# A new order, other PSUM banks and three rewritten steps in the opening of an attention and two-MLP kernel

## The chip, the cores and the metric

The kernel runs on one core of a Trainium2 chip, in one launch. The metric is device time in microseconds: the time from the start to the end of one execution. Before the change the median of three executions is 849.32 us (847.17 to 850.44).

## What is computed

```python
a = exp(phi - max(phi, axis=2))            # maximum over the sequence
a = a / (sum(a, axis=2) + 1e-9)            # (4, 8, 576, 32)
k_m = einsum('bhsm,bhsd->bhmd', a, k)      # 32 memory slots for each head
v_m = einsum('bhsm,bhsd->bhmd', a, v)
scores = q @ k_m.T / 8                     # (4, 8, 576, 32)
attn = softmax(scores)                     # over the 32 slots
x = (attn @ v_m), heads side by side       # (2304, 512)
h = x @ w_in;  x = (h * sigmoid(h)) @ w_out        # 512 -> 2048 -> 512
out = ((x @ w_a) * (x @ w_b)) @ w_out2             # 512 -> 1536 -> 512
```

q, k, v are (4, 8, 576, 64) and phi is (4, 8, 576, 32), all float32. The weights come as 64-bit floats and are turned into float32 on the chip. The large products are made of three float32r products each, of a high and a low half of both operands.

## The kernel before

The work runs in stages. The **opening** does the attention of the four batches and the first units of the first MLP; then follow the rest of the first MLP, and the second MLP (`ab`, `op`). In the opening a hand-written planner sets the order: each task is a generator that yields its next operation with an engine, an estimated time, what it needs and which buffers it takes or frees. The planner always takes, on the engine that can start first, the operation of the lowest rank that is ready by then. The instructions of each engine keep the order that comes out, and each engine works through its own queue in that order. Ranks are 0 for the loads, 1 for what follows a unit's products, 2 to 8 by batch and weight tile, 8.5 for the units.

For a batch `b` the tasks of the opening are:

- `weights(b)`: phi arrives in tile `ph` (128 rows, 4 x 9 x 32 values a row). VectorE takes the maximum over the nine pieces with four `tensor_tensor` instructions (tiles `m`, `mxa`); TensorE transposes it (`mxt`), VectorE reduces that (`mx`), ScalarE widens it (`mb`), TensorE brings it back (`bc`), VectorE subtracts it (`ph<-ph,bc`), ScalarE takes the exponential.
- `sums(b)`: VectorE adds the nine pieces with four more instructions (`m`, `es`).
- `memory(b)`: TensorE multiplies the exponentials by k and v (`kvp`, 72 products a batch), and `es` by a column of ones (`sm`, 8 products). VectorE takes the reciprocals (`rec`), ScalarE scales (`kvn`); for batches 0 and 1 TensorE transposes the keys (`kt`).
- `values(b)`: the transposed values (`vt`), split into `vbd_hi` and `vbd_lo`.
- `turn(b, hg, n)`, batches 0 and 1: three transposes of the queries each (`qt`), copied by ScalarE to `qT`.
- `scores(b, hg)`: the products `sc`, and then the softmax, nearly all of it on VectorE (`x`, `mxq`, `smq`, `xt`), split at its end into the halves `at` (two tiles for each of the two `hg`; the low half is `at<-xt,at`).
- `vw_first`: the values times the first weights (`mp`), split into `m0h`, `m0l` and so on.
- the units: `hp` products of `at` with the tiles `m0h`, `m0l`, then `g`, `gh`, `gl`, then `yp` products with `wo`.
- `tile_of`: turns a weight tile into float32 with VectorE and ScalarE (`e`, `t`), then into a high half (ScalarE) and a low half (VectorE, `wi_0l`, `wo_0l`, ...).

PSUM is divided into pools of two buffers each: "bank" (`ps_t`: `mp`, `kvp`, `kt`, `vt`), "hp" and "yp". `BANK_W[b]` says from which pool `mxt`, `bc` and `sm` of a batch come, `BANK_Q[b]` the same for `qt`. A buffer is taken again when the instruction that reads it is done; a writer behind it waits. Loads go out on SyncE's queue in the order of `LOADS`; each waits there until its buffer is free, and what stands behind it waits too.

Of the kernel before, what the change touches and what calls it, by code (L numbers as in the profile page):

```python
# [9 lines left out]
F32 = mybir.dt.float32  # L10
# [4 lines left out]
ALU = mybir.AluOpType  # L15
AX = mybir.AxisListType
# [4 lines left out]
def attn_moe_moe2_kernel(  # L21
# [540 lines left out]

    def weights(b):

        yield op("V", 1750, [f"phi{b}"])
        e = st[b]["ph"]

        m4 = p_s.tile([128, 4, 4, NM], F32, tag="m4", name="m4")
        mxa = p_s.tile([128, 4, NM], F32, tag="mxa", bufs=2, name="mxa")
        for o, x, y in (  # L570
            (m4, e[:, :, 0:4], e[:, :, 4:8]), (m4[:, :, 0:2], m4[:, :, 0:2], m4[:, :, 2:4]),
            (m4[:, :, 0], m4[:, :, 0], m4[:, :, 1]), (mxa, m4[:, :, 0], e[:, :, 8]),
        ):
            V.tensor_tensor(out=o, in0=x, in1=y, op=ALU.max)
        yield op("T", 400, take=(BANK_W[b], f"mxt{b}"))
        mxt = bank_of(BANK_W[b], "mxt")[:, :128].rearrange("p (r n) -> p r n", r=2)
        T.transpose(mxt.rearrange("p r n -> p (r n)"), mxa.rearrange("p x m -> p (x m)"), ident)
        yield op("V", 290, free=[f"mxt{b}"])
        mx = p_s.tile([128, 2], F32, tag="mx", bufs=2, name="mx")
        V.tensor_reduce(out=mx, in_=mxt, op=ALU.max, axis=AX.X)  # L580

        yield op("A", 300)
        mb = p_s.tile([128, 2, 64], F32, tag="mxa", bufs=2, name="mb")
        A.activation(out=mb, in_=mx.unsqueeze(2).to_broadcast([128, 2, 64]), func=AF.Copy)
        yield op("T", 500, take=(BANK_W[b], f"bc{b}"))
# [7 lines left out]
    def sums(b):

        yield op("V", 1800, [f"w{b}"], done=f"es{b}")
        e = st[b]["ph"]
        m4 = p_s.tile([128, 4, 4, NM], F32, tag="m4", name="m4")
        es = st[b]["es"] = p_s.tile([128, 4, NM], F32, tag="mxa", bufs=2, name="es")
        for o, x, y in (
            (m4, e[:, :, 0:4], e[:, :, 4:8]), (m4[:, :, 0:2], m4[:, :, 0:2], m4[:, :, 2:4]),  # L600
            (m4[:, :, 0], m4[:, :, 0], m4[:, :, 1]), (es, m4[:, :, 0], e[:, :, 8]),
        ):
            V.tensor_tensor(out=o, in0=x, in1=y, op=ALU.add)

    def memory(b):

        t = st[b]
        for hg in range(2):
            yield op("T", 2070, [f"w{b}", f"kv{b}{hg}"], take=("bank", f"kvp{b}") if hg == 0 else None,
                     free=[f"kv{b}{hg}"] + [f"ph{b}"] * hg)  # L610
            e = t["ph"]
            if hg == 0:
                kvp = ps_t.tile([128, 2, 2 * D], F32, tag="t", name="kvp")
            kv = t.pop(("kv", hg))
            for c in range(JP):
                for h in range(4):

                    o = slice(32 * h, 32 * h + 32)
                    x, r = (h // 2 + b) % 2, slice(64 * (h % 2), 64 * (h % 2) + 64)
                    T.matmul(  # L620
                        kvp[o, hg], e[r, 2 * hg + x, c], kv[r, :, x, c * D : c * D + D], start=(c == 0), stop=(c == JP - 1)
                    )
        yield op("T", 250, [f"es{b}"], take=(BANK_W[b], f"sm{b}"))
        sm = bank_of(BANK_W[b], "sm")[:, :2]
        for hg in range(2):
            for h in range(4):
                x, r = (h // 2 + b) % 2, slice(64 * (h % 2), 64 * (h % 2) + 64)
                T.matmul(sm[32 * h : 32 * h + 32, hg : hg + 1], t["es"][r, 2 * hg + x], ones[r, :1])
        yield op("V", 350, free=[f"sm{b}"])
        rec = p_s.tile([128, 2], F32, tag="mx", bufs=2, name="rec")  # L630
        V.tensor_scalar_add(rec, sm, EPS)
        V.reciprocal(out=rec, in_=rec)
        yield op("A", 950, [f"vt{b - 1}"] if b else [], done=f"kvn{b}", take=("kvn", f"kvn{b}"), free=[f"kvp{b}"])

        kvn = t["kvn"] = p_s.tile([128, 2, 4, D], F32, tag="kvn", name="kvn")
        for hg in range(2):
            A.activation(
                out=kvn[:, hg].rearrange("p (a r) d -> p a r d", r=2),
                in_=kvp[:, hg, : 2 * D].rearrange("p (a d) -> p a d", a=2).unsqueeze(2).to_broadcast([128, 2, 2, D]),
                func=AF.Copy, scale=rec[:, hg : hg + 1],  # L640
            )
        if b in NEW:

            yield op("T", 500, done=f"kmT{b}", take=("bank", f"kt{b}"))
            kt = ps_t.tile([128, 2, 128], F32, tag="t", name="kt")
            for hg in range(2):
                T.transpose(kt[:, hg], kvn[:, hg, 0:2].rearrange("p a d -> p (a d)"), ident)
            yield op("A", 400, done=f"kT{b}", take=("kT", f"kT{b}"), free=[f"kt{b}"])
            t["kT"] = p_s.tile([128, 2, 128], F32, tag="kT", bufs=2, name="kT")
            A.activation(out=t["kT"], in_=kt, func=AF.Copy)  # L650
            return
        yield op("V", 350, done=f"kmT{b}")
        kmT = t["kmT"] = p_s.tile([128, 2, 2, NM], F32, tag="kmT", bufs=2, name="kmT")
        V.transpose(out=kmT.rearrange("p g e m -> p g (e m)"), in_=kvn[:, :, 0])
        yield op("A", 1250, [f"sc{b - 1}0", f"sc{b - 1}1"] if b > 2 else [], done=f"kbd{b}")
        for h in range(4):
            r = slice(32 * h, 32 * h + 32)
            A.activation(out=kbd[r, :, :, r], in_=kmT[r], func=AF.Copy)
# [94 lines left out]
    def tile_of(what, c):  # L753
# [26 lines left out]
        V.tensor_tensor(out=ti, in0=ti, in1=ei, op=ALU.add)  # L780
        yield op("A", 650, free=[f"e_{name}"])
        copy(A, hi, t)
        yield op("V", 700, done=name, free=[f"t_{name}"])
        V.tensor_tensor(out=lo, in0=t, in1=hi.bitcast(F32), op=ALU.subtract)
        (wi if what == "wi" else wo)[0, c] = hi, lo

    def loads():
# [78 lines left out]
    def feed_forward():  # L866
        for n, u in enumerate(UNITS):
# [3 lines left out]
            for c in range(4):  # L871
                if c < len(cs):
                    key = f"{n}_{c}"
                    rings["g"][1].append("gg" + key)
                    yield op("T", 800, [f"at{b}0", f"at{b}1", f"m{b}0{halves}", f"m{b}1{halves}"]
                             + ([("free", rings["g"][1][-9])] if len(rings["g"][1]) > 8 else []),
                             take=("hp", "hp" + key),
                             free=[f"m{b}0", f"m{b}1"] if last and c == len(cs) - 1 else [])
                    hp = mul_h(u, cs[c])
                    add(1, g_task(u, cs[c], hp, key), free_at["T"])  # L880
                if n:
                    w = UNITS[n - 1]
                    key = f"{n - 1}_y{c}"
                    yield op("T", 400 * len(w[3]), [f"g{n - 1}_{i}" for i in range(len(w[3]))] + [f"wo{i}" for i in w[3]],
                             take=("yp", key), free=[f"gg{n - 1}_{i}" for i in range(len(w[3]))] if c == 3 else [])
                    yp = mul_y(w, c)
                    add(1, y_task(w, c, yp, key), free_at["T"])
                tick()
                due(0)
            done.add((f, b, hf))  # L890
# [6 lines left out]


    LOADS = (
        "wi00 q00 phi00 wo00 kv00 wi01 q01 kv01 wo01 phi10 q10 wi02 kv11 kv10 q11 wi03 q20 wo03 phi20 wo02 q21 kv20 phi30 q30 kv21 q31 kv31 kv30"  # L900
    ).split()
    NEW = (0, 1)
    RANK = (2, 5, 7, 8)
    RANK_I = (3, 3, 5, 4)
    RANK_O = (4, 4, 2, 6)
    BANK_W = ("yp", "yp", "hp", "hp")
    BANK_Q = ("yp", "bank", "bank", "bank")
    fill()
    add(0, loads())
    add(8.5, feed_forward())  # L910
    for b in range(B):
        add(RANK[b], weights(b))
        add(RANK[b], memory(b))
        add(RANK[b], sums(b))
        add(RANK[b], values(b))
        for hg in range(2):
            for n in range(3 * (b in NEW)):
                add(RANK[b], turn(b, hg, n))
            add(RANK[b], scores(b, hg))
        for kc in range(2):  # L920
            if b == 0:
                add(3, vw_first(0, kc, (0,)))
                add(5, vw_first(0, kc, (1,)))
            else:
                add(RANK[b], vw_first(b, kc, (0, 1)))
    for c in range(4):
        add(RANK_I[c], tile_of("wi", c))
        add(RANK_O[c], tile_of("wo", c))
    run(range(9))
    run((1, 8.5))  # L930
    pinned[0] = False
    for p in (ps_sc, ps_t, ff["h"], ff["y"], p_c, p_s, p_in):
        p.release()
# [356 lines left out]
```

## Time and profile before

| | |
|---|---|
| median of three executions | 849.32 us |
| the profiled execution, its own time | 846.86 us |
| its span, first to last instruction | 845.1 us |
| TensorE busy (PE) | 804.0 us, 95% |
| VectorE busy (DVE) | 571.3 us, 68% |
| ScalarE busy (ACT) | 470.9 us, 56% |
| GpSimd busy (POOL) | 72.4 us, 9% |

The page's busy row for TensorE, in slices of about 21 us, is `6584989999...`: only the first seven slices or so are below nine tenths. The page's chain of work that ended last is TensorE for 84%. A share over the whole span says little about the opening, so the rows further down are of stretches and single instructions there. A row of the timeline gives the start, the duration, the engine, the operation, output <- inputs, shapes and a count; in brackets the idle time of the engine ahead of it and what ended it.

### The profile page before, as it was taken

How to read it: one execution, taken by the hardware profiler on the slowest of the kernel's cores; microseconds unless marked ns; L12 is line 12 of the kernel's file. 1: busy time of each engine (PE TensorE's matmuls, PEld its weight loads, DVE VectorE, ACT ScalarE, POOL GpSimd, SP SyncE). 2: the span in 40 equal slices, each digit the busy share in tenths (PEclk: the TensorE clock that was granted, in tenths of full speed). 3: DMA queues.
4: the chain of work that ended last, by engine and by line, in shares of the span. 5: the costliest groups of instructions: out<-in, count | busy, mean ns of one | idle time of the engine just before them, and what ended most of it. 6: DMA issues, size and time to landing. Idle time of an engine off the chain costs nothing.

```text
span 845.1 us, 14031 instructions
## 1 busy us (share of the span) xinstructions
PE 804.0 (95%) x5460; PEld 759.6 (90%) x5460; DVE 571.3 (68%) x1116; ACT 470.9 (56%) x947; POOL 72.4 (9%) x87
## 2 busy tenths in 40 slices
PE   6584989999999999999999999999999999999998
PEld 5374889999999999999989999999999999999996
DVE  5998776877677667767598886586664874543534
ACT  4574667996676567867456775645443553222220
POOL 1000000211010001122001101101010110100000
PEclk8697999999999999999999999999999999999999
DMA  9752601235331333355287779979785985756653
GB/s 338 218 205 78 224 1 51 75 101 126 100 88 38 85 92 88 79 121 116 41 318 249 249 236 284 256 251 266 219 238 159 279 234 162 195 178 200 198 157 75
DMA packets 59956, 140.91 MB, mean 167 GB/s; under 512 B 5233, under 2 KB 30321, under 8 KB 59889
## 3 DMA queue, kind: packets, MB, share of 16 engines
q1 hardware_dynamic: 48512, 122.44, 44.4%
q0 software_dynamic: 10224, 17.04, 12.0%
q8 instruction: 43, 0.70, 0.3%
q10 hardware_dynamic: 1152, 0.52, 0.3%
q14 instruction: 25, 0.20, 0.1%
HBM read 101.71 MB, written 21.23 MB: 145 GB/s over the span
## 4 chain that ended last, share of the span: by engine, by line
PE 84%; ACT 7%; DVE 6%; DMA 2%; issue 1%; ACTq 0%; DVEq 0%
PE ab L69 30%; PE yp L69 19%; PE op L69 18%; PE hp L69 9%; PE mp L69 3%; PE kvp L69 2%; PE sc L69 1%; ACT g L69 1%; ACT gh L69 1%; DVE t_wi L69 1%; DVE x L69 1%; DMA st_b<-in_moe_w_b_dram 1%; ACT L69 1%; ACT e_wo L69 1%; DVE smq L69 1%
## 5 line engine op out<-in xcount | busy, mean ns | idle before, releaser
L69 PE MATMUL ab<-yq,wh 128*128 128x384 f32 x1080 | 260.7, 338 | 2.0 <-DVE yq L69 1.2
L69 PEld LDWEIGHTS ab<-yq,wh 128*128 128x128 f32 x1080 | 196.5, 189 | 9.1 <-DVE yq L69 1.5
L69 PE MATMUL ab<-yq,wl 128*128 128x384 f32 x432 | 146.3, 339 | 0.0
L69 ACT ACTIVATE u<-ab 128x384 f32<-128x384 f32 x108 | 52.3, 490 | 87.1 <-PE ab L69 86.8
L69 DVE TENSOR_TENSOR gl<-g,gh 128x288 fp32r<-128x288 f32 x128 | 58.9, 464 | 47.2 <-ACT gh L69 46.5
L69 DVE TENSOR_TENSOR y<-op,y 128x512 f32<-128x512 f32 x54 | 37.3, 692 | 78.2 <-PE op L69 77.3
L69 PE MATMUL op<-wol,ph 128*128 128x512 f32 x216 | 85.5, 396 | 0.0
L69 ACT ACTIVATE g<-hp 128x288 f32<-128x288 f32 x128 | 51.9, 409 | 60.1 <-PE hp L69 52.1
L69 PE MATMUL op<-woh,pl 128*128 128x512 f32 x216 | 84.9, 393 | 0.0
L69 PE MATMUL op<-woh,ph 128*128 128x512 f32 x216 | 84.6, 392 | 0.0
L69 PEld LDWEIGHTS ab<-yq,wl 128*128 128x128 f32 x432 | 81.6, 189 | 0.0
L69 ACT ACTIVATE ph<-u 128x384 fp32r<-128x384 f32 x72 | 37.4, 524 | 66.0 <-DVE u L69 60.2
L69 DVE TENSOR_TENSOR u<-ab,u 128x384 f32<-128x384 f32 x108 | 59.8, 556 | 20.6 <-PE ab L69 19.6
L69 DVE TENSOR_TENSOR y<-yp,y 128x288 f32<-128x288 f32 x104 | 47.4, 456 | 29.2 <-PE yp L69 28.6
L69 ACT ACTIVATE gh<-g 128x288 fp32r<-128x288 f32 x128 | 55.9, 443 | 2.7
L69 PEld LDWEIGHTS op<-woh,pl 128*128 128x128 f32 x216 | 40.6, 188 | 9.0
L69 PEld LDWEIGHTS op<-woh,ph 128*128 128x128 f32 x216 | 40.6, 188 | 6.7
L69 PEld LDWEIGHTS op<-wol,ph 128*128 128x128 f32 x216 | 40.5, 188 | 6.4
L69 DVE TENSOR_TENSOR pl<-u,ph 128x384 fp32r<-128x384 f32 x72 | 39.2, 551 | 2.0 <-ACT ph L69 1.8
L69 PE MATMUL hp<-at,m0h 128*128 128x288 f32 x128 | 27.9, 309 | 11.1 <-DVE ph L69 11.1
L69 PE MATMUL yp<-gh,wo_0h 128*128 128x288 f32 x128 | 38.1, 298 | 0.3 <-ACT y L69 0.3
L69 PE MATMUL yp<-gh,wo_2h 128*128 128x288 f32 x128 | 38.1, 297 | 0.1
(218 smaller groups left out, 1887.5 us busy)
## 6 DMA issues: line engine op xcount, KB each, us to landing
yq<-yd SPq DMA_DIRECT2D x63, 768.0 KB, 4.8
yd<-yq SPq DMA_DIRECT2D x21, 768.0 KB, 4.4
st_wi<-in_moe_w_in_dram SPq DMA_DIRECT2D x16, 512.0 KB, 4.3
st_wo<-in_moe_w_out_dram SPq DMA_DIRECT2D x16, 512.0 KB, 3.8
st_a<-in_moe_w_a_dram SPq DMA_DIRECT2D x12, 512.0 KB, 6.1
st_b<-in_moe_w_b_dram SPq DMA_DIRECT2D x12, 512.0 KB, 5.6
wl<-s POOLq DMA_DIRECT2D x24, 256.0 KB, 6.1
st_o<-in_moe_w_out_dram SPq DMA_DIRECT2D x12, 512.0 KB, 6.0
```

What stands on the lines that cost most here:

```text
L69: ins = f(*a, **k)
```

## The change

- `weights`: the four maxima become one `tensor_reduce` over a rearranged view of `ph`, so that the nine pieces are read with a stride of 32 values.
- `sums` is gone. `memory` forms the sum with 72 products of the exponentials with the column of ones (`sm`), added up in PSUM over the nine pieces; `ph` is freed only behind them.
- `tile_of`: the low half of the four `wo` tiles of the opening is made by GpSimd; that of the `wi` tiles stays on VectorE.
- The ranks become a table `R` with a number of its own for each task, the order of the loads is another, and `BANK_W` and `BANK_Q` name other pools. All tasks, the ones after the units' products too, are run by one call.

```diff
-        for o, x, y in (
-            (m4, e[:, :, 0:4], e[:, :, 4:8]), (m4[:, :, 0:2], m4[:, :, 0:2], m4[:, :, 2:4]),
-            (m4[:, :, 0], m4[:, :, 0], m4[:, :, 1]), (mxa, m4[:, :, 0], e[:, :, 8]),
-        ):
-            V.tensor_tensor(out=o, in0=x, in1=y, op=ALU.max)
+        V.tensor_reduce(out=mxa, in_=e.rearrange("p x c m -> p x m c"), op=ALU.max, axis=AX.X)
...
-        yield op("T", 250, [f"es{b}"], take=(BANK_W[b], f"sm{b}"))
+        yield op("T", 1100, take=(BANK_W[b], f"sm{b}"), free=[f"ph{b}"])
         sm = bank_of(BANK_W[b], "sm")[:, :2]
         for hg in range(2):
-            for h in range(4):
-                x, r = (h // 2 + b) % 2, slice(64 * (h % 2), 64 * (h % 2) + 64)
-                T.matmul(sm[32 * h : 32 * h + 32, hg : hg + 1], t["es"][r, 2 * hg + x], ones[r, :1])
+            for c in range(JP):
+                for h in range(4):
+                    x, r = (h // 2 + b) % 2, slice(64 * (h % 2), 64 * (h % 2) + 64)
+                    T.matmul(
+                        sm[32 * h : 32 * h + 32, hg : hg + 1], e[r, 2 * hg + x, c], ones[r, :1],
+                        start=(c == 0), stop=(c == JP - 1), skip_group_check=True,
+                    )
...
-        yield op("V", 700, done=name, free=[f"t_{name}"])
-        V.tensor_tensor(out=lo, in0=t, in1=hi.bitcast(F32), op=ALU.subtract)
+        eng, ns, g = ("V", 700, V) if what == "wi" else ("G", 1500, GP)
+        yield op(eng, ns, done=name, free=[f"t_{name}"])
+        g.tensor_tensor(out=lo, in0=t, in1=hi.bitcast(F32), op=ALU.subtract)
...
-        "wi00 q00 phi00 wo00 kv00 wi01 q01 kv01 wo01 phi10 q10 wi02 kv11 kv10 q11 wi03 q20 wo03 phi20 wo02 q21 kv20 phi30 q30 kv21 q31 kv31 kv30"
+        "wo00 phi00 kv00 wi00 wi01 kv01 wo01 q00 phi10 q01 kv11 q11 wi03 wo03 q10 q21 kv10 wi02 phi20 kv21 q20 kv20 phi30 wo02 q31 q30 kv31 kv30"
...
-    RANK = (2, 5, 7, 8)
...
-    BANK_W = ("yp", "yp", "hp", "hp")
-    BANK_Q = ("yp", "bank", "bank", "bank")
...
+        weights=(44, 26, 4, 36), memory=(14, 0, 39, 41), values=(16, 33, 18, 21), turn0=(1, 35, 32, 8),
...
+    BANK_W = ("yp", "hp", "yp", "yp")
+    BANK_Q = ("yp", "yp", "hp", "bank")
```

What the new numbers do to the order, at three places. First TensorE, ahead of the first `hp` products (`at_67` and its like are the halves of batch 0's softmax; `qt` are the transposed queries, `bc` is the maximum of batch 1 on its way back, `sc` the scores of batch 0):

```order
 L69 MATMUL mp<-wi_1l,vbd_hi_83 128x256
 L69 MATMUL mp<-wi_1h,vbd_lo_85 128x256
-L69 MATMUL sc<-qT,kT 32x288 x8
-L69 MATMUL qt<-ident,qq 128x128 x9
+L69 MATMUL qt<-ident,qq 128x128 x12
+L69 MATMUL bc<-ident,mb 128x128
+L69 MATMUL qt<-ident,qq 128x128 x6
 L69 MATMUL hp<-at_67,m0h 128x288
 L69 MATMUL hp<-at_75,m0h 128x288
```

The scores have moved further ahead, and batch 1's `bc` and all its `qt` now stand ahead of the first `hp`. Right behind the first two groups of `hp`, TensorE too:

```order
 L69 MATMUL hp<-at_76,m0h 128x288
 L69 MATMUL hp<-at_68,m0l 128x288
-L69 MATMUL bc<-ident,mb 128x128
-L69 MATMUL qt<-ident,qq 128x128 x6
 L69 MATMUL kvp<-kv,ph 32x128 x72
+L69 MATMUL sm<-ones,ph 32x1 x72
+L69 MATMUL mxt<-ident,mxa 128x128
 L69 MATMUL mp<-wi_3h,vbd_hi_83 128x256
 L69 MATMUL mp<-wi_3l,vbd_hi_83 128x256
```

Batch 1's `kvp` follows `hp` at once, and the 72 products with ones follow `kvp`. The last place is VectorE at the end of batch 1's softmax, where batch 2's maximum is subtracted (`ph<-ph,bc`). Before:

```order
L69 TENSOR_TENSOR x<-x,smq 128x576 x2
L69 STREAM_TRANSPOSE xt<-x 128x576 x2
L69 TENSOR_TENSOR at_77<-xt,at_69 128x576
L69 TENSOR_TENSOR at_78<-xt,at_70 128x576
L69 TENSOR_TENSOR wo_3l<-t_wo_757,wo_3h 128x512
L69 TENSOR_TENSOR ph<-ph,bc 128x1152
L69 STREAM_TRANSPOSE qT<-qq 128x1152
```

and after the change:

```order
L69 TENSOR_REDUCE mx<-mxt 128x2
L69 TENSOR_REDUCE smq<-x 128x18
L69 TENSOR_SCALAR smq<-smq 128x18
L69 RECIPROCAL smq<-smq 128x18
L69 ISA t_wo_991<-t_wo_991,e_wo_977 128x1024
L69 TENSOR_TENSOR x<-x,smq 128x576
L69 TENSOR_TENSOR ph<-ph,bc 128x1152
L69 STREAM_TRANSPOSE xt<-x 128x576
```

The subtraction stood behind both low halves of batch 1's softmax (`at_77`, `at_78`); now it stands six rows behind batch 2's `mx`, ahead of both.

## Rows read from the trace of the kernel before

**Rows 1.** Busy times by stretch: engines, granted clock, DMA share, GB/s

```profile
0.00:76.40 76.40, 44.18 (x578) 37.01 (x579) 63.80 (x134) 43.23 (x89) 4.21 (x12) 0.82 0.64 210
76.40:130.00 53.60, 50.91 (x580) 46.75 (x581) 38.74 (x83) 34.46 (x69) 0.00 (x0) 0.94 0.37 119
130.00:400.00 270.00, 269.93 (x1981) 266.59 (x1980) 188.32 (x384) 196.80 (x420) 33.82 (x37) 1.00 0.37 89
```

**Rows 2.** Timeline of TensorE in the opening, single rows

```profile
0.97 4.57 PE L69 MATMUL jk<-ones 128*96 128x96 f32 x32 [0.97 <-POOL ones L69]
...
14.67 3.81 PE L69 MATMUL kvp<-kv,ph 64*32 64x128 f32 x72 [2.64 <-ACT ph L69]
...
20.02 2.17 PE L69 MATMUL kvp<-kv,ph 64*32 64x128 f32 x72
22.01 0.28 PE L69 MATMUL sm<-ones,es 64*32 64x1 f32 x16
...
38.43 2.38 PE L69 MATMUL qt<-ident,qq 128*128 128x128 f32 x9 [8.51 <-DVE m0l L69]
...
76.41 0.82 PE L69 MATMUL hp<-at,m0h 128*128 128x288 f32 x2 [11.09 <-DVE ph L69]
```

**Rows 3.** Timeline of VectorE in the opening, single rows

```profile
6.22 0.69 DVE L69 SCALAR_TENSOR_TENSOR t_wi<-e_wi,t_wi 128x512 uint32<-128x512 uint32 x1
...
8.24 0.69 DVE L69 TENSOR_TENSOR m<-ph 128x512 f32<-128x512 f32 x1
...
9.96 0.68 DVE L69 TENSOR_TENSOR wi_0l<-t_wi,wi_0h 128x512 fp32r<-128x512 f32 x1
...
22.69 0.15 DVE L69 TENSOR_SCALAR rec<-sm 128x2 f32<-128x2 f32 x1
...
26.18 0.72 DVE L69 TENSOR_TENSOR vbd_lo<-vt,vbd_hi 64x64 fp32r<-64x64 f32 x4
...
38.82 0.76 DVE L69 TENSOR_TENSOR at<-xt,at 128x576 fp32r<-128x576 f32 x1
...
74.92 1.35 DVE L69 TENSOR_TENSOR ph<-ph,bc 128x1152 f32<-128x1152 f32 x1
```

**Rows 4.** Busy times between the two softmaxes' ends, columns as in rows 1

```profile
39.60:74.50 34.90, 22.62 (x309) 19.88 (x307) 33.29 (x72) 24.72 (x52) 0.00 (x0) 0.89 0.40 133
```

**Rows 5.** Busy times in the slow-clock stretches; sums of the first three, the last two

```profile
31.80:41.90 10.10, 3.47 (x15) 3.13 (x16) 9.66 (x19) 4.23 (x8) 0.00 (x0) 0.50 0.44 96
sum 20.15, PE 10.88 PEld 8.69 DVE 18.30 ACT 8.59 POOL 0.00; mean PE 3.63 PEld 2.90 DVE 6.10 ACT 2.86 POOL 0.00
...
sum 6.40, PE 6.40 PEld 6.01 DVE 6.23 ACT 4.87 POOL 0.00; mean PE 3.20 PEld 3.00 DVE 3.11 ACT 2.43 POOL 0.00
```

**Rows 6.** DMA issues at 1.26 and 4.41 us: count, size, us to landing

```profile
qq<-in_q_dram SPq DMA_DIRECT2D x1, 576.0 KB, 4.7
...
qq<-in_q_dram SPq DMA_DIRECT2D x1, 576.0 KB, 10.3
```

**Rows 7.** Groups on VectorE, 0 to 130 us: count, busy us, mean ns, idle

```profile
L69 DVE TENSOR_REDUCE mxq<-x 128x18 f32<-128x576 f32 x8 | 5.9, 734 | 0.1
L69 DVE TENSOR_REDUCE mx<-mxt 128x2 f32<-128x128 f32 x4 | 1.1, 283 | 0.0
```

**Rows 8.** Chain of work that ended last: start, us, what; then TensorE's timeline

```profile
24.84 1.21 PE sc L69 x16
...
83.94 0.80 PE hp L69 x6
...
94.17 2.21 PE L69 MATMUL sc<-qT,kbd 128*128 128x288 f32 x8
```

**Rows 9.** Timelines of GpSimd and VectorE near 151 us, and a VectorE group

```profile
150.68 1.62 POOL L69 TENSOR_TENSOR wi_1l<-t_wi,wi_1h 128x512 fp32r<-128x512 f32 x1 [1.62 <-ACT wi_1h L69]
...
151.06 1.56 DVE L69 TENSOR_TENSOR gl<-g,gh 128x288 fp32r<-128x288 f32 x1
...
L69 DVE TENSOR_TENSOR gl<-g,gh 128x288 fp32r<-128x288 f32 x16 | 7.2, 452 | 2.1 <-ACT gh L69 1.8
```

More of the change, by code (lines that the diff above doesn't have):

```diff
@@ L563, in weights @@
     def weights(b):
-        yield op("V", 1750, [f"phi{b}"])
+        yield op("V", 1350, [f"phi{b}"])
         e = st[b]["ph"]
-        m4 = p_s.tile([128, 4, 4, NM], F32, tag="m4", name="m4")
         mxa = p_s.tile([128, 4, NM], F32, tag="mxa", bufs=2, name="mxa")
-        for o, x, y in (
-            (m4, e[:, :, 0:4], e[:, :, 4:8]), (m4[:, :, 0:2], m4[:, :, 0:2], m4[:, :, 2:4]),
-            (m4[:, :, 0], m4[:, :, 0], m4[:, :, 1]), (mxa, m4[:, :, 0], e[:, :, 8]),
-        ):
-            V.tensor_tensor(out=o, in0=x, in1=y, op=ALU.max)
+        V.tensor_reduce(out=mxa, in_=e.rearrange("p x c m -> p x m c"), op=ALU.max, axis=AX.X)
         yield op("T", 400, take=(BANK_W[b], f"mxt{b}"))
@@ L591, in weights @@
         A.activation(out=e, in_=e, func=AF.Exp)
[L593 to L603, printed above, removed]
     def memory(b):
@@ L609, in memory @@
             yield op("T", 2070, [f"w{b}", f"kv{b}{hg}"], take=("bank", f"kvp{b}") if hg == 0 else None,
-                     free=[f"kv{b}{hg}"] + [f"ph{b}"] * hg)
+                     free=[f"kv{b}{hg}"])
             e = t["ph"]
@@ L879, in feed_forward @@
                     hp = mul_h(u, cs[c])
-                    add(1, g_task(u, cs[c], hp, key), free_at["T"])
+                    add(R["g"][0], g_task(u, cs[c], hp, key), free_at["T"])
                 if n:
@@ L886, in feed_forward @@
                     yp = mul_y(w, c)
-                    add(1, y_task(w, c, yp, key), free_at["T"])
+                    add(R["y"][0], y_task(w, c, yp, key), free_at["T"])
                 tick()
@@ L899, in attn_moe_moe2_kernel @@
     LOADS = (
-        "wi00 q00 phi00 wo00 kv00 wi01 q01 kv01 wo01 phi10 q10 wi02 kv11 kv10 q11 wi03 q20 wo03 phi20 wo02 q21 kv20 phi30 q30 kv21 q31 kv31 kv30"
+        "wo00 phi00 kv00 wi00 wi01 kv01 wo01 q00 phi10 q01 kv11 q11 wi03 wo03 q10 q21 kv10 wi02 phi20 kv21 q20 kv20 phi30 wo02 q31 q30 kv31 kv30"
     ).split()
     NEW = (0, 1)
-    RANK = (2, 5, 7, 8)
-    RANK_I = (3, 3, 5, 4)
-    RANK_O = (4, 4, 2, 6)
-    BANK_W = ("yp", "yp", "hp", "hp")
-    BANK_Q = ("yp", "bank", "bank", "bank")
+    R = dict(
+        weights=(44, 26, 4, 36), memory=(14, 0, 39, 41), values=(16, 33, 18, 21), turn0=(1, 35, 32, 8),
+        turn1=(36, 23, 13, 30), scores0=(9, 37, 43, 15), scores1=(24, 45, 3, 2), vw0=(19, 38, 42, 28),
+        vw1=(5, 40, 25, 27), first=(22, 26), wi=(10, 34, 17, 29), wo=(6, 20, 12, 31), units=(37,), g=(11,),
+        y=(7,),
+    )
+    BANK_W = ("yp", "hp", "yp", "yp")
+    BANK_Q = ("yp", "yp", "hp", "bank")
     fill()
     add(0, loads())
-    add(8.5, feed_forward())
+    add(R["units"][0], feed_forward())
     for b in range(B):
[L912 to L915, printed above, removed]
+        add(R["weights"][b], weights(b))
+        add(R["memory"][b], memory(b))
+        add(R["values"][b], values(b))
         for hg in range(2):
             for n in range(3 * (b in NEW)):
-                add(RANK[b], turn(b, hg, n))
-            add(RANK[b], scores(b, hg))
+                add(R[f"turn{hg}"][b], turn(b, hg, n))
+            add(R[f"scores{hg}"][b], scores(b, hg))
         for kc in range(2):
             if b == 0:
-                add(3, vw_first(0, kc, (0,)))
-                add(5, vw_first(0, kc, (1,)))
+                add(R["first"][kc], vw_first(0, kc, (0,)))
+                add(R[f"vw{kc}"][0], vw_first(0, kc, (1,)))
             else:
-                add(RANK[b], vw_first(b, kc, (0, 1)))
+                add(R[f"vw{kc}"][b], vw_first(b, kc, (0, 1)))
     for c in range(4):
[L927 to L930, printed above, removed]
+        add(R["wi"][c], tile_of("wi", c))
+        add(R["wo"][c], tile_of("wo", c))
+    run()
     pinned[0] = False
```

## The prediction

> **What bounds the kernel now.** I read the busy times by stretch first [rows 1]. From 130 us on TensorE does not stop (269.93 of 270 us), and from 76.4 to 130 it has 50.91 of 53.6. Up to 76.4 it has only 44.18. So whatever the change is worth lies in the opening: the time at the end is the moment from which TensorE no longer runs dry, plus the TensorE work still left then, plus the little that is lost later.
>
> Then TensorE's own rows [rows 2]. Two stops make up 19.6 us: the transposes `qt` at 38.43 had waited 8.51 us for VectorE's `m0l`, and `hp` at 76.41 had waited 11.09 us for VectorE's `ph`. Both are PSUM buffers whose reader was late. The first is in the pool "bank": batch 1's `qt` needs a buffer that holds batch 0's `mp`, and its reader `m0l` stands on VectorE behind nearly the whole softmax of batch 0, which ends with the low half at 38.82 + 0.76 = 39.58 [rows 3]. The second is in the pool "hp": batch 2's `bc` holds it, and its reader `ph<-ph,bc` starts at 74.92 [rows 3], behind the softmax of batch 1. VectorE meanwhile is full: 33.29 busy of 34.90 us from 39.6 to 74.5 [rows 4].
>
> Stops also cost clock. The granted clock is 0.50 (the 1.2 GHz level) from 31.8 to 41.9, most of which TensorE had stood idle. In the three such stretches ahead of 76.4 it was busy 10.88 us, in the two behind it 6.40 us [rows 5]; at the 2.4 GHz level the same work takes half, so 5.44 and 3.20 us are lost.
>
> In a sum, with W for all of TensorE's work at the upper level: before 76.4 it has done 44.18 - 5.44 = 38.74; later it loses 53.6 - 50.91 = 2.69 idle and 3.20 by the clock. T(before) = 76.4 + (W - 38.74) + 2.69 + 3.20 = W + 43.55, and what comes after 130 us is the same on both sides.
>
> **The change, part by part.** I lay the change's order end to end with the durations of these rows.
>
> Start. The second transfer lands at 1.26 + 4.7 = 6.0 us [rows 6]; it is now phi. VectorE's three steps on the first weight tile end at 6.22 + 0.69 = 6.91 as before, then comes the reduce; before, the four maxima ran from 8.24 to 9.96 [rows 3], 1.72 us. No row shows a reduce of 1152 elements, nor one that reads with a stride. By elements, 128 take 283 ns and 576 take 734 [rows 7], 1.01 ns for each more, so 1.31 us; 2.6 if the stride doubles it. I take 1.31, since the rows of its own kind lie on that line. One weight step follows it on VectorE in both kernels. So `kvp` starts 1.33 + 0.41 = 1.7 us earlier, at 13.0 for 14.67 [rows 2].
>
> Batch 0's memory. Before, its halves took 3.81 and 2.17 us with a pause between [rows 2]. The new load order makes kv01 the eighth transfer; the eighth landed at 4.41 + 10.3 = 14.7 [rows 6], ahead of its use at 16.8. So no pause: it ends at 13.0 + 5.98 = 19.0. The sums then come from TensorE. TensorE's rows count passes, two to a product here. An `sm` pass lasts 0.167 us alone, and 16 took 0.28 [rows 2], so one follows another by (0.28 - 0.167)/15 = 7.6 ns. A batch has 144 passes for 16: 1.27 us, 0.98 more than before. Bounds: 17.5 ns each if the whole 0.28 counts, 30 ns at `kvp`'s pace (2.17/72); hardly below 7.6. I take 7.6, the row of the same instruction. `rec` starts at 20.3 for 22.69. From there to the end of the scores took 24.84 + 1.21 - 22.69 = 3.36 [rows 3, 8]; the softmax starts at 23.7, and VectorE is free for it: ahead of it are only three steps of 0.7 to 1.3 us. Before, it waited for `vbd_lo` and started at 26.9.
>
> Batch 0's softmax took 26.9 to 39.58, 12.7 us. In the new order `vbd_lo` (0.76), batch 1's `mx` (0.2) and its `ph<-ph,bc` (1.28 net) stand inside it: 14.9. With 0.4 for handovers, the last low half is done at **39.0**, hardly earlier than before. What differs is what else is ready by then: all 36 `qt` are done, since they no longer share a pool with `mp`, and batch 1's weights are through their exponential, so `kvp` of batch 1 follows the first `hp` at once.
>
> TensorE's work done by 39.0: the warming `jk` 4.57, 72 `kvp` 4.34, `sm` 1.27, 36 `qt` at 2.38/9 halved 4.8, twelve `mp` 1.4, scores 1.2, eight small ones 1.2, four `hp` 0.5 (0.80 for six [rows 8]; `mp` by its columns, 256 for 288), and 1.7 for the ends of runs that the busy time holds too: 21.0.
>
> From there it must not run dry until batch 1's softmax is done. The order puts 80 VectorE instructions between the two batches' last low halves. At the 0.46 us of [rows 4] (33.29/72) that is 37; the two reduces and two `qT` among them are 0.9 longer each: 40.5. TensorE has in that stretch 216 `kvp` (13.0), 144 `sm` (2.2), 116 `hp` and `yp` (15.5), 48 `mp` (5.7), scores 1.2 + 2 x 2.21 [rows 8] and ten small ones (1.5): 43.5 us. It is covered, by 3 us. The trap of the second stop is gone too: batch 2's `bc` is now in "yp", and its reader stands a few rows behind the reader of its `mxt`.
>
> The rest: `sums` takes 1.7 us per batch off VectorE (6.9 in all) and the four low halves some 2.5; these are in the 80 instructions already. What TensorE takes on, 4 x 0.98 = 3.9 us, is paid in full, because it is now the bound. Later losses: 1.5 by the clock just behind 39.0, as in [rows 5], and 1.0 idle.
>
> T(after) = 39.0 + (W + 3.9 - 21.0) + 2.5 = W + 24.4. The difference is 24.4 - 43.55 = **-19.2 us**. The profiled execution took 846.86, so it would take 827.7; that execution was 2.5 below the median of 849.32, which becomes **830.2**.
>
> GpSimd. A subtraction like the moved ones ran at 150.68 for 1.62 us, and VectorE's `gl` beside it took 1.56 for the usual 0.452 [rows 9]: 1.1 us lost. If each of the four does so, VectorE loses 4.4 us and is spared 2.5. GpSimd itself has time: behind its first fills it stands idle through the opening. The Trainium skill ("SBUF — State Buffer", section "Who interferes with whom") says that a VectorE instruction with two SBUF inputs contends with a GpSimd instruction that reads SBUF, and that the loser blocks for the whole instruction. That row agrees, and by the rule the move costs VectorE more than it saves.
>
> **The rivals.**
> Forecast: TensorE runs through from 39 us. For it: the 43.5 against 40.5 us. 830.2; 826 to 836 with its unknowns (a slower reduce 1.3 twice, `sm` at 17.5 ns 512 x 9.9 = 5.1; the clock staying up from 39 us, -1.5).
>
> VectorE still binds. The cover is 3 us. GpSimd's 4.4, taken on instructions in the stretch, and waits like those of [rows 4] (34.90 - 33.29 = 1.6) would use it up twice: TensorE stops for some 3 us, and loses as much again by the clock. 836. (The Trainium skill's rule in "SBUF — State Buffer" is the one that would bring this about.) Against: only three of the four fall in the stretch, and many VectorE instructions there read PSUM.
>
> A load is late. SyncE issues batch 1's first keys behind the last queries, which wait for a `qq` buffer until batch 1's third `qt` is copied. By my walk the keys land about 1.4 us before they are needed; each us beyond that is a us at the end. Some 3 us: 833, inside the range of the two above.
>
> Slower than before: the ones products. They load new weights for each column; if a pass cost 45 ns or more (six times the row), 512 of them would take 23 us and eat everything; at `kvp`'s pace on the lower clock, 3.81/72 = 53 ns, 27 us less the 3.9 counted: 853. Against: the 7.6 ns are measured with weights of the same form.
>
> It does nothing: the two stops return at other buffers. "yp" now holds `mxt`, `bc`, `sm` and `qt`, with two buffers. If a reader is queued as before, 8.5 and 11.1 us come back: 849.
>
> **How the numbers follow.** Forecast 0.70, VectorE or a load binds 0.22, nothing 0.04, slower 0.04. Nothing in the first two is under 0.5% (4.2 us, about what can be told from no change here). So faster 0.92, same 0.04, slower 0.04. The range 824 to 839 takes in the first two with their bounds: down to a clock that stays up and a chain 4 us shorter, up to `sm` at 17.5 ns and 3 us of stops at once.
>
> **What would show it.** Right: no TensorE stop over 3 us after 39 us, batch 1's `kvp` near 40, 144 `sm` rows in about 1.3 us, PEclk 1.00 from about 45 us. Wrong: a stop of `hp` for `at` or `ph` between 60 and 85 us (VectorE binds), `sm` runs over 2.5 us, or `kvp` of batch 1 waiting for a transfer.

## The result and the profile after

The changed kernel takes **840.69 us** (median of 4 runs, 839.7 to 842.02), the kernel before, on the same chip, 849.11 (4 runs, 847.17 to 850.44). The ratio is 0.9904 with a 95% interval of 0.988 to 0.9927: faster by 8.4 us, 1.0%. Forecast were 830.2, with 824 to 839: the direction holds, but less than half of the gain came, and the time lies 1.7 us above the range. The profiled execution of after took 842.02 us, with a span of 840.2; that of before took 846.86.

Busy times of the changed kernel by stretch (columns as in [rows 1]), the last line being the stretch of [rows 4]:

```profile
0.00:130.00 130.00, 110.35 (x1713) 98.16 (x1713) 100.93 (x191) 79.99 (x162) 9.32 (x16) 0.86 0.51 175
...
130.00:400.00 270.00, 269.76 (x1974) 265.89 (x1975) 188.48 (x385) 194.69 (x420) 34.24 (x37) 1.00 0.37 91
...
39.60:74.50 34.90, 30.62 (x511) 27.10 (x510) 27.82 (x49) 21.79 (x46) 1.27 (x1) 0.82 0.62 209
```

TensorE has 110.35 us busy up to 130 where before it had 44.18 + 50.91 = 95.09 [rows 1]: some 15 us of idle time are gone. VectorE is down from 33.29 to 27.82 in the stretch that it filled before [rows 4]; it binds no longer. But the granted clock of the 130 us is 0.86; TensorE works more of the time, and more of that at the lower level.

What it still waits for, in the list of waits (engine, tile and line, what released it: us in all, times, the longest), 0 to 130 us:

```profile
PE sm L69 <- issue: 3.6, 2, 2.5
PE mxt L69 <- DVE mxa L69: 3.4, 2, 3.3
PE yp L69 <- issue: 2.7, 1, 2.7
PE kvp L69 <- ACT ph L69: 2.6, 1, 2.6
```

The two long stops of [rows 2] are gone. "issue" is new: time in which TensorE waited for nothing that the profile shows. Its timeline has the three places, each in or behind a run of the new ones products:

```profile
19.54 0.56 PE L69 MATMUL sm<-ones,ph 64*32 64x1 f32 x42
21.13 1.02 PE L69 MATMUL sm<-ones,ph 64*32 64x1 f32 x102 [1.03 <-issue]
...
50.63 1.41 PE L69 MATMUL sm<-ones,ph 64*32 64x1 f32 x144
57.17 0.40 PE L69 MATMUL yp<-gl,wo_0h 128*128 128x288 f32 x1 [2.67 <-issue]
...
77.82 1.10 PE L69 MATMUL sm<-ones,ph 64*32 64x1 f32 x113
81.45 0.43 PE L69 MATMUL sm<-ones,ph 64*32 64x1 f32 x31 [2.52 <-issue]
```

The second run goes through in 1.41 us, as forecast (1.27). The first stops after 42 passes, the third after 113, and behind the second it is a `yp` that stands for 2.67 us. The fourth, at 106.70 us, goes through in 1.37. That is 6.2 us of stops, and behind the two longer ones the clock is at 0.50 (58.80 to 62.21 us, 82.69 to 86.10).

The page's list of DMA queues has a queue that loads instructions. Its lines before and after (packets, MB, share of the engines' time), and that of after from 54 to 58 us alone:

```profile
q8 instruction: 43, 0.70, 0.3%
```

```profile
q8 instruction: 47, 0.77, 0.4%
```

```profile
q8 instruction: 1, 0.02, 1.7%
```

Four packets more, of 0.77 MB / 47 = 16 KB each. TensorE has 4 x 64 = 256 products more, of two passes each, and each pass is two instructions, a load of weights and a product: 1024 instructions, 256 to a packet. One packet starts 2.2 to 2.7 us ahead of the end of each of the three stops (taken in steps of 0.2 us, at 18.4, 54.8 and 79.0 us). This suggested theory F: a run of tiny products uses up instructions faster than they are fetched. The experiments put it against rivals: that only the work of the added products counts (P), that VectorE or its dear reduce binds (D), that GpSimd blocks VectorE (G).

**An account of TensorE's time.** For each kernel, up to 130 us: what TensorE stood idle, and half of what it was busy in the stretches with a clock of 0.50, which is what those cost.

| kernel | idle, us | lost by the clock, us | sum |
|---|---|---|---|
| before | 34.9 | 8.9 | 43.8 |
| after | 19.7 | 15.4 | 35.0 |
| after, 8 ones products a batch (`e1_sm8`) | 15.6 | 6.6 | 22.2 |
| after, sums on GpSimd (`e8_gsum`) | 18.0 | 8.4 | 26.4 |
| after, ones products spread (`e4_mixed`) | 29.8 | 7.2 | 37.0 |
| before with the ones products (`e15_ones`) | 41.2 | 11.4 | 52.6 |

From before to after the sum falls by 8.7, the 512 added passes cost 3.9: -4.8 us, and the two profiled executions differ by 4.84. In the same terms the prediction left the changed kernel 18.0 us up to 39 (39.0 less the 21.0 of work) and 2.5 later, 20.5 in all. Measured are 35.0. With the runs of tiny products cut out it is 22.2, so 12.8 of the 14.5 us that are missing hang on them. (In medians 10.5 are missing and not 14.5: the profiled execution of after lies 1.3 us above its median, and that of before 2.2 below.)

### The profile page after: what moved, and what is told of

It is laid out like the page before. It is cut to its first block, busy times and chain, and to the rows that moved or that the text cites. A ratio compares the mean times of both kernels' runs of the same rounds, so it can differ in the third digit from the quotient of the medians.

```text
span 840.2 us, 15039 instructions
## 1 busy us (share of the span) xinstructions
PE 814.1 (97%) x5972; PEld 768.4 (91%) x5972; DVE 566.6 (67%) x1084; ACT 468.2 (56%) x945; POOL 77.1 (9%) x91
## 3 DMA queue, kind: packets, MB, share of 16 engines
q10 hardware_dynamic: 1152, 0.52, 0.3%
## 4 chain that ended last, share of the span: by engine, by line
PE 87%; DVE 4%; issue 4%; ACT 2%; DMA 2%; POOL 0%; POOLq 0%
PE ab L69 30%; PE yp L69 21%; PE op L69 18%; PE hp L69 11%; PE kvp L69 2%; PE mp L69 2%; PE sc L69 1%; DMA st_b<-in_moe_w_b_dram 1%; PE sm L69 1%; DVE x L69 1%; DVE mxa L69 1%; ACT L69 0%; DVE yq L69 0%; DVE smq L69 0%; DMA wo_2l<-t_wo 0%
## 5 line engine op out<-in xcount | busy, mean ns | idle before, releaser
L69 PE MATMUL yp<-gl,wo_0h 128*128 128x288 f32 x128 | 38.0, 297 | 2.7 <-issue 2.7
L69 PE MATMUL yp<-gh,wo_2l 128*128 128x288 f32 x128 | 38.0, 297 | 0.2 <-DMA wo_2l<-t_wo 0.2
```

The source lines that it names most:

```text
L69: ins = f(*a, **k)
```

## The experiments

All times are medians; each was compared with runs of the kernel before on the same chip (848.1 to 849.1).

**One product in nine.** The same kernel, in the same order, with 8 ones products a batch.

```diff
-            for c in range(JP):
+            for c in range(1):
                 for h in range(4):
...
-                        start=(c == 0), stop=(c == JP - 1), skip_group_check=True,
+                        start=True, stop=True, skip_group_check=True,
```

> The changed kernel with the ones products of one piece in nine: 8 products a batch where there were 72, in the same places of the same order. The sum in the denominator then holds one ninth of the terms; nothing else is left out. Theory F (a run of 144 tiny passes takes TensorE's instructions faster than they are fetched, so TensorE stands for 1.0, 2.7 and 2.5 us in and behind these runs and loses clock behind each stop): the work of 4 x 0.98 = 3.9 us goes, the 6.2 us of stops go, and some 3 us of clock: about 13 us faster than the changed kernel, near 828; no wait on TensorE without a releaser between 15 and 90 us, and no longer 0.50 clock behind 57 and 81 us. Rival P (only the work of the added products counts, the stops have another cause): 3.9 us faster, near 837, and the stops at 57 and 81 us are still there. Rival D (VectorE binds after all): under 2 us faster.

Measured: **826.85 us** (826.65 to 827.18; ratio to before 0.9744, 0.9725 to 0.9763), 13.8 less than the changed kernel. No wait on "issue" is left, and the queue of instructions is back at 43 packets:

```profile
0.00:130.00 130.00, 114.39 (x1312) 103.29 (x1312) 111.47 (x211) 91.99 (x191) 12.21 (x18) 0.93 0.54 181
```

```profile
q8 instruction: 43, 0.70, 0.3%
```

Theory F gave 13, P 3.9, D under 2. Idle time falls by 4.0 and the loss by the clock by 8.8 (the table), the work by 3.9; that is 16.7 for the 15.1 between the two profiled executions, since this kernel stands 1.8 us longer between 400 and 800 us (3.84 idle for 2.08).

**The price by itself.** 512 more tiny products at the very start, where TensorE has nothing to do, with one moving column and with 96.

```diff
         warm_up(ones, WARM)
+        jt = ff["y"].tile([128, W], F32, tag="yp", name="jt")
+        for n in range(512):
+            o, r = 32 * (n % 4), 64 * (n % 2)
+            T.matmul(jt[o : o + 32, :1], ones[r : r + 64, :32], ones[r : r + 64, :1], start=True, stop=True)
```

(In the second run `:96` in the result and all 96 columns of `ones` as the moving operand.)

> The changed kernel with 512 more products of 64 rows, 32 columns of weights and one moving column behind the warming ones, at the very start, where TensorE has nothing else to do until 8 us; their result is not used. It measures the price of such a run by itself: 1024 passes. Rival P: 7.6 ns each, 7.8 us in one piece. Theory F: the passes come in bundles of some 125 with stops between; at 2.3 to 2.5 us from one fetch to the end of the stop, 2048 instructions or 8 packets take 18 us or more; at the 1.05 us that a packet's transfer takes, 8.4 us.

> The changed kernel with 512 more products behind the warming ones as in the run with tiny ones, but with 96 moving columns in place of one; their result is not used. Theory F with the prices seen there (256 instructions in 6.5 us while loads fill the transfer engines, 3.6 us when they are still): 128 passes take some 3 us of work at the upper clock, so they still come in bundles of 128, 6.5 us apart at first and 3.6 us apart once the loads rest, and the whole takes as long as with one column, from 6 to 38 us. Rival (the tiny products are slow by their form, not by their number): no stops, 512 x 2 x 25 ns = 26 us in one piece.

Measured: 870.35 and 870.1 us, one execution each. TensorE's timeline with one moving column, then DMA's share in three stretches of it (the share is the last column but one), and the queue:

```profile
6.08 1.75 PE L69 MATMUL jt<-ones 64*32 64x1 f32 x191
12.59 1.88 PE L69 MATMUL jt<-ones 64*32 64x1 f32 x128 [4.76 <-issue]
19.06 1.88 PE L69 MATMUL jt<-ones 64*32 64x1 f32 x128 [4.59 <-issue]
22.51 1.88 PE L69 MATMUL jt<-ones 64*32 64x1 f32 x128 [1.57 <-issue]
...
37.15 1.04 PE L69 MATMUL jt<-ones 64*32 64x1 f32 x65 [1.85 <-issue]
```

```profile
12.50:19.00 6.50, 1.88 (x128) 1.80 (x128) 0.00 (x0) 0.00 (x0) 0.00 (x0) 0.50 1.05 398
19.00:38.00 19.00, 10.25 (x704) 9.84 (x704) 0.00 (x0) 0.00 (x0) 0.00 (x0) 0.50 0.06 20
```

```profile
q8 instruction: 55, 0.90, 0.4%
```

Bundles of exactly 128 passes, 256 instructions, with stops between; 8 packets more than in the changed kernel for 2048 instructions. A packet's worth takes 6.5 us while the loads fill the transfer engines (share 1.05) and 3.6 us when they are still (share 0.06: five bundles from 19.06 to 37.15). On the queue a packet starts 2.2 to 2.7 us ahead of each bundle. Per pass that is **28 to 51 ns**, where a short run showed 7.6. Theory F's 18 us or more became 32; the 2.3 to 2.5 us from a fetch to the end of a stop, from which it was worked out, is not the whole of what a packet takes.

With 96 columns the stops shrink and the bundles come within 1.1 us of the same times:

```profile
13.10 4.22 PE L69 MATMUL jt<-ones 64*32 64x96 f32 x128 [2.85 <-issue]
19.30 7.13 PE L69 MATMUL jt<-ones 64*32 64x96 f32 x256 [1.97 <-issue]
26.76 2.84 PE L69 MATMUL jt<-ones 64*32 64x96 f32 x128 [0.32 <-issue]
...
37.94 1.56 PE L69 MATMUL jt<-ones 64*32 64x96 f32 x65 [0.61 <-issue]
```

The runs end at 38.2 and 39.5 us, with 14.0 and 24.2 us of busy time between 6 and 38. From 19 to 38 us the granted clock was 0.50 in the first and 0.91 in the second, so the clock does not set the pace either. So it is the number of instructions that counts and not what each does. The rival (26 us in one piece) falls.

**The same products, spread.** Each ones product right behind the `kvp` product of its piece.

```diff
...
-        yield op("T", 1100, take=(BANK_W[b], f"sm{b}"), free=[f"ph{b}"])
...
                     T.matmul(
-                        sm[32 * h : 32 * h + 32, hg : hg + 1], e[r, 2 * hg + x, c], ones[r, :1],
+                        sm[o, hg : hg + 1], e[r, 2 * hg + x, c], ones[r, :1],
                         start=(c == 0), stop=(c == JP - 1), skip_group_check=True,
                     )
+        yield op("T", 1100, free=[f"ph{b}"])
```

> The changed kernel with the same 72 ones products of each batch, but each right behind the kvp product of the same piece and head, so that no 144 tiny passes stand in a row. The PSUM buffer of the sums is taken 6 us earlier. Theory F (a run of tiny passes outruns the fetch of instructions): 512 instructions then take some 5.5 us, a packet's 256 in 2.7 us, longer than the 2.3 to 2.5 us from a fetch to the end of a stop, so the stops of 1.0 and 2.5 us at the runs shrink below 0.5 each, and the changed kernel becomes some 5 us faster, near 835. Rival P (the number of passes alone): the same time within 1 us. Rival B (the buffer held longer costs a wait): slower by 1 us or more, with TensorE's mxt, bc, qt or yp waiting for VectorE's rec.

Measured: 843.32 us (842.01 to 844.21), 2.6 more than the changed kernel: the forecast of both theories missed. From the list of waits:

```profile
PE qt L69 <- DMA qq<-in_q_dram: 5.1, 1, 5.1
PE yp L69 <- DVE rec L69: 3.8, 1, 3.8
PE kvp L69 <- issue: 3.5, 4, 1.1
...
PE kt L69 <- issue: 2.3, 1, 2.3
PE sm L69 <- issue: 1.5, 1, 1.5
```

Spread, 256 of these instructions are used up in an estimated 2.4 us at the upper clock ((30 + 7.6) ns x 64), still less than the 3.6 us that a packet takes, so the stops come back: four at `kvp` (3.5 us together), one of 2.3 and one of 1.5, 7.3 us in all. The expectation rested on 2.3 to 2.5 us a packet, which the run before has replaced. Besides, the buffer held longer costs its own wait (`yp` for `rec`, 3.8), as rival B said, and a later `qt` waits 5.1 us for queries.

**The sums elsewhere.** Eight products a batch again, the additions over the nine pieces on VectorE (`e3_vsum`) or on GpSimd (`e8_gsum`), issued where `kvp` is.

```diff
+                m4 = p_s.tile([128, 4, 4, NM], F32, tag="m4", name="m4")
+                es = p_s.tile([128, 4, NM], F32, tag="es", bufs=2, name="es")
+                for o, x, y in (
+                    (m4, e[:, :, 0:4], e[:, :, 4:8]), (m4[:, :, 0:2], m4[:, :, 0:2], m4[:, :, 2:4]),
+                    (m4[:, :, 0], m4[:, :, 0], m4[:, :, 1]), (es, m4[:, :, 0], e[:, :, 8]),
+                ):
+                    GP.tensor_tensor(out=o, in0=x, in1=y, op=ALU.add)
```

> The changed kernel with the sum over the nine pieces back on VectorE (four additions on a batch, set into its order where kvp is issued) and 8 ones products a batch, the rest of the order as it was. Theory F: the stops without a releaser go, as with 8 products alone (826.9), and VectorE pays 4 x 1.72 = 6.9 us, of which batch 0's lie beside kvp and are free; of the other three, VectorE is waited for in the stretch up to the second softmax: 2 to 4 us lost, so 829 to 831, some 10 us faster than the changed kernel. Rival D (VectorE binds): the 6.9 us come back in full, 834 or more.

> The changed kernel with the sum over the nine pieces on GpSimd (four additions on a batch, beside kvp, which needs 4.3 us or more) and 8 ones products a batch, the rest of the order as it was. Theory F: the stops without a releaser go, VectorE has nothing to pay, and if the additions end before kvp, the time is that of 8 products alone, 827; by up to 1.1 us longer for each batch if GpSimd blocks VectorE beside it (theory G), up to 831. Rival: the additions take longer than kvp, and sm waits for GpSimd: 830 or more, with sm waiting for es in the list of waits.

Measured: 832.61 us on VectorE (831.76 to 834.34), **830.17 on GpSimd** (829.78 to 831.02; ratio to before 0.9791, 0.9774 to 0.9807). GpSimd's additions end ahead of `kvp` (16.92 + 0.78 for 13.97 + 6.16), and `sm` does not wait for GpSimd:

```profile
14.00 1.39 POOL L69 TENSOR_TENSOR m<-ph 128x512 f32<-128x512 f32 x1 [2.37 <-ACT ph L69]
15.46 1.38 POOL L69 TENSOR_TENSOR m<-m 128x256 f32<-128x256 f32 x2
16.92 0.78 POOL L69 TENSOR_TENSOR es<-m,ph 128x128 f32<-128x128 f32 x1
```

```profile
13.97 6.16 PE L69 MATMUL kvp<-kv,ph 64*32 64x128 f32 x144 [2.64 <-ACT ph L69]
19.96 0.27 PE L69 MATMUL sm<-ones,es 64*32 64x1 f32 x16
```

So the whole sums are to be had at 830.2 us, 10.5 under the changed kernel and 18.8 under the kernel before: a version that beats both. The 3.3 us above `e1_sm8` are partly GpSimd's doing: VectorE's instruction beside the additions of batch 1 took 1.65 us where its like takes 0.69 (VectorE's timeline, then GpSimd's row beside it):

```profile
42.18 1.65 DVE L69 SCALAR_TENSOR_TENSOR t_wi<-e_wi,t_wi 128x512 uint32<-128x512 uint32 x1
...
51.34 0.69 DVE L69 SCALAR_TENSOR_TENSOR t_wi<-e_wi,t_wi 128x512 uint32<-128x512 uint32 x1
```

```profile
42.01 1.27 POOL L69 TENSOR_TENSOR m<-ph 128x512 f32<-128x512 f32 x1 [14.40 <-issue]
```

On VectorE the sums cost 2.4 us more than on GpSimd, and 5.8 more than `e1_sm8`: theory F was right that the stops go (none on "issue" is left), but the time lies between its 829 to 831 and rival D's 834: of the 6.9 us of VectorE's work it let only 2 to 4 come back. With the stops gone VectorE is waited for again, 33.53 of 34.90 us busy (`e3_vsum`, columns as in [rows 1]):

```profile
39.60:74.50 34.90, 30.95 (x483) 27.41 (x483) 33.53 (x64) 25.52 (x53) 2.76 (x2) 0.94 0.76 251
```

**The low halves back on VectorE.**

```diff
-        g.tensor_tensor(out=lo, in0=t, in1=hi.bitcast(F32), op=ALU.subtract)
+        V.tensor_tensor(out=lo, in0=t, in1=hi.bitcast(F32), op=ALU.subtract)
```

> The changed kernel with the four low halves of the first weights back on VectorE, everything else in its order. Theory G (a GpSimd subtraction blocks VectorE by 1.1 us): the four took VectorE 4.4 us by blocking and now cost it 2.5, so 1 to 2 us faster than the changed kernel. Theory F (TensorE's instructions bind in that stretch, and GpSimd's 1.27 us steps block little): VectorE has 2.5 us more to do, the time within 1 us of the changed kernel's 840.7, the stops of 2.7 and 2.5 us as before.

Measured: 840.46 us (839.74 to 841.68), the changed kernel's time within 0.3. Theory G falls for these four.

**The maximum.** Over neighbouring elements (`e2_flat`), by the four steps of before in the changed kernel (`e14_max4`), and by the four steps in the kernel with the sums on GpSimd (`e9_gsum_max4`).

```diff
-        V.tensor_reduce(out=mxa, in_=e.rearrange("p x c m -> p x m c"), op=ALU.max, axis=AX.X)
+        V.tensor_reduce(
+            out=mxa, in_=e.rearrange("p x c m -> p (x c m)").rearrange("p (x m c) -> p x m c", x=4, c=JP), op=ALU.max, axis=AX.X
+        )
```

> The changed kernel with the maximum over nine neighbouring elements instead of nine elements 128 bytes apart: the same 1152 elements read and 128 written, in the order in which they lie. The maxima are then those of other groups; nothing else is changed. If the stride is what made the reduce 2.18 us long, it falls to 1.31 us (the line through 128 and 576 elements); if it is the count of elements or of results, it stays near 2.2. The time: if the reduce is on the path at the start, 0.9 us at batch 0 and up to 0.9 more at each later batch while VectorE is waited for: 1 to 3 us faster than the changed kernel; if what TensorE waits for is elsewhere, no difference over 1 us.

> The changed kernel with the maximum by the four steps of the kernel before, everything else as changed. The reduce took 2.18 us, the steps 1.72. Theory F (the fetch of instructions sets the stretch): 0.5 to 1.5 us faster than the changed kernel's 840.7, with the stops of 2.7 and 2.5 us still there, some microseconds earlier. Rival D (the dear reduce is what cost the 10 us): 4 us faster or more.

> The kernel with the sums on GpSimd (830.2) and, besides, the maximum by the four steps of the kernel before in place of the one reduce: 1.72 us for 2.18, 0.46 less on each of four batches. If VectorE's chain at the start is still the path to the first softmax, and VectorE is waited for until the second, 0.5 to 1.5 us faster than 830.2; if TensorE does not wait for VectorE any more, no difference over 0.5 us.

Measured: 839.79, 840.73 and 830.36 us. The groups of the reduce (count, busy us, mean ns, idle), first of the changed kernel, then of `e2_flat`:

```profile
L69 DVE TENSOR_REDUCE mxa<-ph 128x128 f32<-128x1152 f32 x4 | 8.7, 2180 | 0.0
```

```profile
L69 DVE TENSOR_REDUCE mxa<-ph 128x128 f32<-128x1152 f32 x4 | 5.3, 1336 | 0.0
```

It is the stride that makes it dear: 0.84 us of 2.18. But sparing 0.84 or 0.46 us four times over is worth 0.9 and 0.0 us, neither of them clear of noise, and theory F's 0.5 to 1.5 us for `e14_max4` did not come: in `e14_max4` the stop of `yp` on "issue" is still there (3.1 us) and a `qt` waits 3.3 us for its queries. D falls.

**One part undone: the bank table.** The q transposes back in the pools of before.

```diff
-    BANK_Q = ("yp", "yp", "hp", "bank")
+    BANK_Q = ("yp", "bank", "bank", "bank")
```

> The changed kernel with the q transposes of batches 1 and 2 back in the pool bank that kvp and mp use (the table of before), the order drawn up anew from the same ranks. It tests where the gain came from: the forecast put it on two buffers that were held too long. If that is so, stops of TensorE on a buffer return, 8 us or more between 40 and 130 us, and the time is 849 or more, no better than before the change. If the gain came from the lighter VectorE or the new load order, it stays within 3 us of the changed kernel's 840.7.

Measured: 847.6 us (10 runs, 846.79 to 849.93; ratio to before 0.9988, 0.9973 to 1.0003): 6.9 of the 8.4 us are gone again. So the expectation held for the time nearly (849 or more), and not for the stops: no single one of 8 us came back; TensorE's idle time up to 130 us rose from 19.7 to 26.8, in pieces:

```profile
PE kt L69 <- issue: 3.1, 1, 3.1
PE kvp L69 <- ACT ph L69: 2.6, 1, 2.6
PE qt L69 <- DVE m0l L69: 2.3, 2, 1.2
PE kvp L69 <- DMA kv<-in_v_dram: 2.0, 1, 2.0
```

The gain hangs on this table. That it works through the release of the buffer alone is not shown, since the planner draws up another order with it.

**One part alone: the ones products in the kernel before.** Its order as it was, the additions taken out of VectorE, 72 products in place of 8.

```diff
-            for h in range(4):
-                x, r = (h // 2 + b) % 2, slice(64 * (h % 2), 64 * (h % 2) + 64)
-                T.matmul(sm[32 * h : 32 * h + 32, hg : hg + 1], t["es"][r, 2 * hg + x], ones[r, :1])
+            for c in range(JP):
+                for h in range(4):
+                    ...
```

> The kernel before with one part of the change alone: the sums by 72 ones products a batch, the four additions of a batch taken from VectorE, all else in the order of before. By the step of the prediction: VectorE binds in the opening of before, so up to 1.72 us a batch are won in the two or three batches ahead of 76 us, less 0.98 a batch on TensorE, which has 19.6 us of stops to take them: 845 to 849. Theory F: the products of the first batches run into the fetch and each costs 1 to 2.7 us of stop and clock behind it; 849 to 853.

Measured: **862.28 us** (861.25 to 864.96; ratio 1.017, 1.0144 to 1.0195), 14.1 slower than before on the same chip (848.13), further than both theories had it. From its list of waits:

```profile
PE hp L69 <- DVE ph L69: 11.1, 1, 11.1
PE qt L69 <- DVE m0l L69: 8.5, 1, 8.5
PE kvp L69 <- ACT ph L69: 4.6, 2, 2.6
PE sm L69 <- issue: 4.1, 3, 2.8
...
PE sc L69 <- issue: 1.7, 1, 1.7
...
PE yp L69 <- issue: 1.1, 1, 1.1
```

6.9 us of stops on "issue", 3.9 of work, 2.5 more by the clock (the table); and the two old stops are as long as ever although VectorE has up to 1.72 us less to do on each batch. What the lighter VectorE wins shows in none of these rows.

## Why the prediction was right in direction and wrong in size

- **What bounds it: right.** The two stops are gone, from 39 us no stop lasts over 3 us, and the longest wait on VectorE behind 39 us is 0.6 (`hp` for `at`). Without the runs of tiny products the kernel takes 826.85; the forecast less the 3.9 us that it allowed for them is 826.3. In the profiled executions it is 826.96 for 823.8, so part of this agreement is luck.
- **The step that failed: the `sm` products at 7.6 ns a pass**, so that they would cost 4 x 0.98 = 3.9 us of work and no wait. Measured, that term is 13.8 us (840.69 less 826.85). A row of 16 passes shows how fast TensorE works off 32 instructions that it already holds; the run of 144 at 50.63 us, 1.41 us long, shows the same. It does not show what the next packet of instructions costs. The prediction's sign of being wrong, `sm` runs over 2.5 us, came twice: 2.6 us from 19.54 and 4.1 from 77.82. In its sum the cost stands mostly behind 39 us, where it allowed 1.0 idle and 1.5 by the clock: measured are 7.2 and 7.5, and with 8 products a batch 0.85 and 2.8. Up to 39 us it is 20.3 for 18.0, with 8 products 18.6. At the 28 ns that a steady run needs even without loads, 512 passes cost 512 x (28 - 7.6) = 10.4 us more, and 830.2 becomes 840.6; that this is so near is luck, since against `e1_sm8` only 4.0 us came as idle time and 8.8 as lost clock. The prediction named 30 ns, `kvp`'s pace, as a bound, but its range reaches only to 17.5. With its own upper bound the range would have held the time.
- **The rival that came true in part** is "the ones products", with a chance of 0.04, a condition of 45 ns a pass and a price of 853 at 53 ns. While loads run, a pass costs 51 ns; put alone into the kernel before, the products cost 14.1 us. Its ground (weights loaded for each column) was not the right one: it is the fetch.
- **Clock.** The forecast expected the upper level from about 45 us. Measured is 0.50 up to 48.55, and again from 58.80 to 62.21 and 82.69 to 86.10; 15.4 us are lost up to 130, where `e1_sm8` loses 6.6. How much of it each stop brought can't be read off, as the first stretches also begin at other times in each kernel; and it does not follow the stops alone: `e4_mixed` has 7.3 us of them and loses 7.2 us by the clock.
- **The reduce.** 2.18 us for 1.31: the bounds held, the value taken did not. The line by elements was right (1.34 over neighbours); the stride was the missing 0.84. Worth under 1 us in the end.
- **Start.** `kvp` began at 13.47 us for 13.0, behind the dearer reduce, `rec` at 22.22 for 20.3, of which 1.03 is the stop in `sm`. From `rec` to the end of the scores it took 4.55 us for 3.36, a term that was mis-sized (4.04 in `e1_sm8`): `kt` now stands behind a third group of q transposes, which waits 0.97 us for ScalarE's copies. The softmax began at 26.87 for 23.7, the first `hp` that needs its last low half at 42.69 for 39.0, and `kvp` of batch 1 at 44.91 for some 40. Most of this lateness hangs on the ones products of batch 0 too: with 8 of them `rec` starts at 19.93, the softmax at 24.07, that `hp` at 39.01 and `kvp` at 41.22. TensorE's row of that `hp`, after and in `e1_sm8`:

```profile
42.69 0.61 PE L69 MATMUL hp<-at,m0h 128*128 128x288 f32 x1 [0.58 <-DVE at L69]
```

```profile
39.01 0.61 PE L69 MATMUL hp<-at,m0h 128*128 128x288 f32 x1 [0.58 <-DVE at L69]
```

- **VectorE binds, or GpSimd blocks it.** Neither. 27.82 us busy of 34.90; `gl` took 455 ns in the mean for 452 before [rows 9]; moving the four back changed nothing. No step with both inputs in SBUF, as `gl` in [rows 9], began beside the four: there VectorE read `sc` or `x`, or ran `ph<-ph,bc` (1.35 us, as in [rows 3]), whose `bc` lies in PSUM. The Trainium skill's rule ("SBUF — State Buffer", section "Who interferes with whom") is borne out in `e8_gsum`, where there is more of GpSimd: beside its additions VectorE's step took 1.65 us for 0.69.

## What to carry to other kernels

Count the instructions that a change adds, not only the time of one: where an engine does 256 in less than a packet's 3.6 to 6.5 us, the packets set the pace, and a row of a short run can't show it. A bound that a prediction writes down belongs in its range unless a row excludes it. And work that comes in many tiny products may be cheaper on an engine that stands idle beside them, slow as it is: GpSimd did the sums at 3.3 us in all, where the products cost 13.8.

## What the runs showed of the hardware

- TensorE's instructions come in packets of 16 KB, 256 of them, some 3.6 us apart with the transfer engines almost still (`e5_tiny`, share 0.06) and 6.5 with loads at 398 GB/s. The Trainium skill ("Runtime: NRT & Kernel Launch", section "Instruction fetch mechanics") has the same packets and says that their cost is mostly hidden. The first agrees with 8 packets for 2048 instructions; the second holds for products of 30 ns a pass and more without loads, and not for these.
- TensorE had some two packets in store, an estimate from the instructions that the timeline shows (`e5_tiny`): the first stop in the run of tiny products came after 32 + 191 passes, 446 instructions.
- VectorE's reduce over elements 128 bytes apart took 2.18 us for 1152 elements, over neighbours 1.34 (`e2_flat`).
